# Attention features of batches 1 to 3: nine row blocks in three groups of three, each with its own bias

## The chip, the cores and the metric

The kernel runs on one core of a Trainium2 chip. The metric is the device time of one execution in microseconds (us); lower is better. The value for a kernel is the median of its runs.

## What is computed

Three stages follow each other. Random-feature attention on q, k, v of shape (4 batches, 8 heads, 576 rows, 64 columns) with 128 features, then two feed-forward stages on the 2304 rows of 512 columns that the attention gives.

```python
def phi(x):
    proj = np.einsum('bhsd,md->bhsm', x, omega)
    sq = np.sum(x * x, axis=-1, keepdims=True) / 2.0
    h = proj - sq
    h = h - np.max(h, axis=-1, keepdims=True)
    return np.exp(h) / np.sqrt(m)
q_p, k_p = (phi(q_s), phi(k_s))
kv = np.einsum('bhsm,bhsd->bhmd', k_p, v)
z = np.sum(k_p, axis=2)
num = np.einsum('bhsm,bhmd->bhsd', q_p, kv)
...
h = x @ w_in                                   # (2304, 512) @ (512, 2048)
g = h * (1.0 / (1.0 + np.exp(-1.702 * h)))
x = g @ w_out
...
out = ((x @ w_a) * (x @ w_b)) @ w_out2         # inner width 1536
```

The change touches how `phi` is cut into pieces; the numbers computed are the same.

## The kernel before

The attention works in phases. A phase is one pair of heads of one batch, for k (`kphase32`) or for q (`qphase`): 2 x 576 rows, cut into nine blocks of 128 rows. A batch has four k phases and four q phases. Batch 0 is done first and alone. The attention of batch b (1 to 3) is then run beside the first feed-forward stage of batch b-1 (`ffn1`), whose matmuls keep TensorE busy: the program is written as generators, and each unit of `ffn1` (twelve matmuls of 512 columns) is followed by one step of every attention phase that is live (`run`, `side_step`). A phase begins two steps after the one before it, so several phases are live together. Batch 1 keeps its features in float32 (`e32`), batches 2 and 3 split them into two float16 parts (`e16`). After the attention comes the second feed-forward stage (`ffn2`), which the change does not touch.

`features` (L374 on) is where `phi` is computed. For a group of blocks it takes one bank of PSUM from the pool `ps_att`, whose tag `att` has two banks for all live phases together; the products of the phase's end (`pk` in the k phase, `pn` twice in the q phase) and the transposes of batch 1 take banks of the same two. Into the bank go the projections (TensorE, L415 and L416, two matmuls of 128 columns for a block). VectorE takes the maximum of each row of each block (L481, one instruction for the group), and two small instructions (L487) turn it into the bias: `mh`, then `nb`, one column for a block. ScalarE then does one exponential for a block, straight from the bank (L447). When the last of them is done the bank is free. For batches 2 and 3, `parts` (L453) makes the two float16 parts of a group: one conversion on ScalarE (L457), one subtraction on VectorE (L458).

Before the change the nine blocks make groups of four, four and one. `PAIRS` says over which groups a bias is shared: group 0 has its own, groups 1 and 2 have one in common, which is made only when the maxima of both are there.

```python
GROUPS = [[0, 1, 2, 3], [4, 5, 6, 7], [8]]
PAIRS = [(0,), (1, 2), (1, 2)]
...
if gi - 1 == pair[-1]:
    for o, i0, scale in ((mh, mx, PROJ), (nb, mh, -1.0)):
        own["nb"] = nc.vector.scalar_tensor_tensor(...)
    for gj in pair:
        exps(gj, nb, a)
```

The steps are, before: (1) project group 0; (2) maximum, bias and exponentials of group 0, project group 1; (3) parts of group 0, maximum of group 1, project group 2; (4) maximum of group 2, shared bias, exponentials of groups 1 and 2; (5) parts of groups 1 and 2.

The order on each engine is not the order of the text. The framework's planner lays the instructions of each engine in a fixed order when the kernel is built: the text's order gives the priority, and the planner's own estimate of durations says when an operand or a buffer is there. At run time every engine follows that order and waits where something is late.

Other work on the same engines: VectorE converts weights from the raw form (`w_ops`, L215 to L263), does two instructions for each unit of `ffn1` (L667, L677) and the end of the q phases (L594 to L630). ScalarE does `th` and `gh` of `ffn1` (L664, L672, L676).

Of the kernel before, what the change touches and what calls it, by code (L numbers as in the profile page):

```python
# [9 lines left out]
F32 = mybir.dt.float32  # L10
F16 = mybir.dt.float16
I32 = mybir.dt.int32
AF = mybir.ActivationFunctionType
ALU = mybir.AluOpType
# [8 lines left out]
S_E = 2.0**13  # L23
# [11 lines left out]
def fused_kernel(  # L35
# [13 lines left out]
    nc = tc.nc  # L49
    B, H, S, D = q.shape  # L50
    M = omega.shape[0]
    DM, F1 = w_in_d.shape
    F2 = w_a_d.shape[1]
    P = 128
    NT = 4
# [6 lines left out]
    T = 2 * NT + 1  # L62
# [267 lines left out]


    raws = {}
    GROUPS = [[0, 1, 2, 3], [4, 5, 6, 7], [8]]
    PAIRS = [(0,), (1, 2), (1, 2)]
    GROUPS_F = [[0, 2, 4, 6], [1, 3, 5, 7], [8]]
    PAIRS_F = [(0, 1, 2)] * 3

# [29 lines left out]
    def places(g, shift):  # L367

        if not shift:
            return slice(g[0], g[-1] + 1)  # L370
        return slice(0, 1) if g[0] == 2 * NT else slice(g[0] + 1, g[-1] + 2)

    def features(pool, nm, x, e16, e32, psp, extra, shift=0):

        if nm[1] == "0":
# [3 lines left out]
            pt, pm = psp(), psp()  # L379
# [21 lines left out]
        else:  # L401
# [3 lines left out]
                out=x16[:, :, 1, :], in0=x, scalar=S_QK, in1=x16[:, :, 0, :],  # L405
                op0=ALU.mult, op1=ALU.subtract,
# [3 lines left out]
                out=xt, in_=x16.rearrange("p t j d -> p (t j d)")  # L410
# [28 lines left out]
        def exps(gi, nb, a):  # L439
            g, pv = groups[gi], pvs[gi]  # L440
            gs = slice(g[0], g[-1] + 1, 2 if len(g) > 1 and g[1] - g[0] == 2 else 1)
            if e32 is None:
                e = pool.tile([P, 4, M], F32, tag="e", name=f"e_{nm}_{gi}", bufs=2)
            else:
                e = e32[:, gs, :]
            for u, i in enumerate(g):
                nc.scalar.activation(  # L447
                    out=e[:, u, :], in_=pv[:, u, :], func=AF.Exp,
                    bias=nb[:, i - a : i - a + 1], scale=PROJ,
                )  # L450
            es[gi] = e

        def parts(gi):  # L453
            g, e = GROUPS[gi], es[gi]
            gs = places(g, shift)
            n = len(g)
            nc.scalar.activation(out=e16[:, 0, gs, :], in_=e[:, :n, :], func=AF.Copy, scale=S_E)  # L457
            nc.vector.scalar_tensor_tensor(  # L458
                out=e16[:, 1, gs, :], in0=e[:, :n, :], scalar=S_E, in1=e16[:, 0, gs, :],
                op0=ALU.mult, op1=ALU.subtract,  # L460
            )

        yield
        pvs, es, mxs, done = {}, {}, {}, []
        for gi in range(len(GROUPS) + 2):
            if e32 is None:
                for gj in [x for x in es if x not in done]:
                    parts(gj)
                    done.append(gj)
            if 1 <= gi <= len(GROUPS):  # L470
                g, pv = groups[gi - 1], pvs[gi - 1]
                pair = pairs[gi - 1]
                a, z = groups[pair[0]][0], groups[pair[-1]][-1] + 1
                ms = slice(g[0] - a, g[-1] + 1 - a, 2 if len(g) > 1 and g[1] - g[0] == 2 else 1)
                if pair[0] not in mxs:
                    mxs[pair[0]] = [
                        pool.tile([P, T], F32, tag=t, name=f"{t}_{nm}_{gi}", bufs=2)
                        for t in ("mx", "mh", "nb")
                    ]
                mx, mh, nb = mxs[pair[0]]  # L480
                nc.vector.tensor_reduce(  # L481
                    out=mx[:, ms], in_=pv[:, : len(g), :], axis=AX.X, op=ALU.max
                )
                if gi - 1 == pair[-1]:

                    for o, i0, scale in ((mh, mx, PROJ), (nb, mh, -1.0)):
                        own["nb"] = nc.vector.scalar_tensor_tensor(  # L487
                            out=o[:, : z - a], in0=i0[:, : z - a], scalar=scale, in1=sq[:, a:z],
                            op0=ALU.mult, op1=ALU.subtract,
                        ).ins  # L490
                    for gj in pair:
                        exps(gj, nb, a)
            if nm[1] == "0":
                if gi == 0:
                    for gj in range(len(GROUPS)):
                        pvs[gj] = psp().rearrange("p (t m) -> p t m", m=M)
                    project()
            elif gi < len(GROUPS):
                pvs[gi] = pv = psp().rearrange("p (t m) -> p t m", m=M)
                project(pv, GROUPS[gi])  # L500
            yield
# [46 lines left out]
    def qphase(pool, b, hp, xT, psp, nxt, f32=False):  # L548
        nm = f"q{b}_{hp}"
        bp, br = b % 2, b // 2  # L550
# [3 lines left out]
        if f32:  # L554
            e32 = pool.tile([P, T, M], F32, tag="e16", name=f"e32_{nm}")
            yield from features(pool, nm, raw, None, e32, psp, nxt)
            eq = pool.tile([P, T * P], F32, tag="eqT", name=f"eT32_{nm}")
            eT = eq.rearrange("p (t m) -> p t m", m=P)
            for gi, g in enumerate(GROUPS):
                pt = psp().rearrange("p (t m) -> p t m", m=M)  # L560
                for u, i in enumerate(g):
                    nc.tensor.transpose(pt[:, u, :], e32[:, i, :], own["ident"])
                cp = nc.vector.tensor_copy if gi in EVD else nc.scalar.copy
                cp(eT[:, places(g, 1 - bp), :], pt[:, : len(g), :])
            yield
            scale = 1.0

            def products(o, hh, c):
                nc.tensor.matmul(o, eq[:, c : c + P], own["kv"][:, hp, hh, :], start=True, stop=True)  # L569
        else:  # L570
            e16 = pool.tile([P, 2, T, P], F16, tag="e16", name=f"e16_{nm}")
            yield from features(pool, nm, raw, e16, None, psp, nxt, 1 - bp)
            TP = T * P
            eq = pool.tile([P, 2 * TP], F16, tag="eqT", name=f"eqT_{nm}")
            nc.sync.dma_start_transpose(
                out=eq.rearrange("p (l t m) -> p (l t) m", l=2, m=P),
                in_=e16.rearrange("p l t m -> p (l t m)"),
            )
            yield
            yield  # L580
            scale = S_E * S_KV

            def products(o, hh, c):
                lh, ll = eq[:, c : c + P], eq[:, TP + c : TP + c + P]
                nc.tensor.matmul(o, lh, kvh[:, hp, hh, :], start=True, stop=False)
                nc.tensor.matmul(o, lh, kvl[:, hp, hh, :], start=False, stop=False)
                nc.tensor.matmul(o, ll, kvh[:, hp, hh, :], start=False, stop=True)
# [31 lines left out]
        if b == 0:  # L619
            pt = psp()  # L620
# [4 lines left out]
        else:  # L625
# [5 lines left out]
            out=x16r[rows, br, 1, hp, :], in0=xr, in1=x16r[rows, br, 0, hp, :], op=ALU.subtract  # L631
        )
        yield
        if b:
            nc.sync.dma_start_transpose(
                out=xT[:, hp].rearrange("p l (t c) -> p (l t) c", t=NT),
                in_=x16.rearrange("p l t c -> p (l t c)"),
# [630 lines left out]
```

## Time and profile before

| | |
|---|---|
| median of 3 runs | 897.92 us (897.53 to 898.5) |
| span of the profiled execution (first to last instruction), which is its own time within 0.1 us of the lowest run | 897.5 us |
| TensorE (PE) busy | 874.1 us, 97% |
| VectorE (DVE) busy | 674.2 us, 75% |
| ScalarE (ACT) busy | 457.6 us, 51% |
| mean granted TensorE clock | 0.995 |

How to read it: the profile gives for each engine the time in which it executes something. Matmuls overlap in their pipe, so a matmul of 512 columns has a record of about 0.38 us while the next one starts 0.215 us after it; a busy TensorE can therefore hide short waits. A wait is idle time of an engine before an instruction, put down to whatever ended it. The stretches used below are: up to 79 us mostly batch 0, 79 to 184 us batch 1 beside `ffn1` of batch 0, 184 to 290 us batch 2 beside `ffn1` of batch 1, 290 to 388 us batch 3 beside `ffn1` of batch 2, then the rest of `ffn1`, and `ffn2` from about 485 us.

### The profile page before, as it was taken

What the parts mean: (1) busy time and instruction counts of PE and PEld (TensorE: products, weight loads), DVE (VectorE), ACT (ScalarE), POOL (GpSimd) and SP (SyncE); (2) the same over time, 40 slices, a digit from 0 to 9 for tenths busy, and PEclk for the clock granted to TensorE, in tenths of its full rate; (3) what the DMA queues carried; (4) which work ended last, traced back from release to release, by engine and by line L of the source; (5) the groups of instructions that cost most, each with busy time, mean ns of one, the idle gap of its engine ahead of it and who ended that gap; (6) DMA issues with size and microseconds to landing.
All of it is one profiled execution on the core that took longest, in us unless ns stands there. A gap on an engine that the chain in (4) does not pass through costs nothing.

```text
span 897.5 us, 17366 instructions
## 1 busy us (share of the span) xinstructions
PE 874.1 (97%) x7094; PEld 628.0 (70%) x7094; DVE 674.2 (75%) x1212; ACT 457.6 (51%) x1088; POOL 1.4 (0%) x10
## 2 busy tenths in 40 slices
PE   8999999999999999999999999999999999999997
PEld 6874655645554455444448888888888889888886
DVE  4889999787797787999611179987999557566766
ACT  6777875677656775564323354544443122233221
POOL 0000000000000000000000000000000000000000
PEclk8999999999999999999999999999999999999999
DMA  6945886344674314785401045232332022223312
GB/s 174 251 143 163 223 209 218 95 124 92 129 172 118 74 28 80 136 269 223 141 1 48 16 138 175 108 89 83 130 130 81 3 42 85 83 95 129 77 49 71
DMA packets 129343, 105.35 MB, mean 117 GB/s; under 512 B 97776, under 2 KB 111088, under 8 KB 127216
## 3 DMA queue, kind: packets, MB, share of 16 engines
q1 hardware_dynamic: 128558, 103.66, 41.0%
q8 instruction: 55, 0.90, 0.4%
q10 hardware_dynamic: 706, 0.59, 0.2%
q14 instruction: 24, 0.20, 0.1%
HBM read 71.07 MB, written 17.69 MB: 99 GB/s over the span
## 4 chain that ended last, share of the span: by engine, by line
PE 66%; DVE 17%; ACT 7%; DMA 4%; issue 2%; ACTq 0%; SPq 0%
PE y L690 4%; PE ph L655 4%; PE ph L656 4%; PE y L691 4%; PE ph L657 4%; PE y L692 4%; DMA xt_k<-x_k 3%; PE oA L912 2%; PE oA L910 2%; PE pbA L816 2%; PE pbA L814 2%; PE pbA L815 2%; PE oA L911 2%; PE pa L569 2%; PE paA L814 2%; PE paA L816 2%
## 5 line engine op out<-in xcount | busy, mean ns | idle before, releaser
L691 PE MATMUL y<-gl,w_out 128*128 128x512 f16 (+1 forms) x320 | 114.4, 358 | 0.6 <-DVE gl L677 0.4
L692 PE MATMUL y<-gh,w_out 128*128 128x512 f16 (+1 forms) x320 | 114.3, 358 | 0.0
L690 PE MATMUL y<-gh,w_out 128*128 128x512 f16 (+1 forms) x320 | 112.3, 358 | 0.7 <-ACT gh L676 0.7
L677 DVE SCALAR_TENSOR_TENSOR gl<-th,gh 128x512 f16<-128x512 f32 (+1 forms) x80 | 50.7, 635 | 66.6 <-ACT gh L676 66.3
L655 PE MATMUL ph<-xT,w_in 128*128 128x512 f16 x256 | 97.0, 379 | 1.5 <-DMA xT<-x_q_3x 0.7
L656 PE MATMUL ph<-xT,w_in 128*128 128x512 f16 x256 | 97.0, 379 | 0.3 <-DVE xT L624 0.3
L657 PE MATMUL ph<-xT,w_in 128*128 128x512 f16 x256 | 97.0, 379 | 0.0
L814 PE MATMUL paA<-forms,w_a 128*128 128x256 f16 (+1 forms) x240 | 61.0, 262 | 1.6 <-DVE ca L835 1.3
L814 PE MATMUL pbA<-forms,w_b 128*128 128x256 f16 (+1 forms) x240 | 61.0, 262 | 0.7 <-DVE cb L835 0.7
L816 PE MATMUL pbA<-forms,w_b 128*128 128x256 f16 (+1 forms) x240 | 61.0, 262 | 0.0
L815 PE MATMUL pbA<-forms,w_b 128*128 128x256 f16 (+1 forms) x240 | 61.0, 262 | 0.0
L816 PE MATMUL paA<-forms,w_a 128*128 128x256 f16 (+1 forms) x240 | 61.0, 262 | 0.0
L815 PE MATMUL paA<-forms,w_a 128*128 128x256 f16 (+1 forms) x240 | 61.0, 262 | 0.0
L912 PE MATMUL oA<-w_o,ab 128*128 128x256 f16 x216 | 58.9, 273 | 0.6 <-DVE ab L868 0.5
L910 PE MATMUL oA<-w_o,ab 128*128 128x256 f16 x216 | 58.9, 273 | 0.1
L911 PE MATMUL oA<-w_o,ab 128*128 128x256 f16 x216 | 58.9, 273 | 0.0
L676 ACT ACTIVATE gh<-th 128x512 f16<-128x512 f32 (+1 forms) x80 | 47.1, 589 | 23.0 <-DVE th L667 22.0
L824 ACT COPY ka<-paA 128x512 f32<-128x512 f32 (+1 forms) x30 | 16.3, 544 | 82.1 <-PE paA L816 82.1
L918 DVE SCALAR_TENSOR_TENSOR o<-oA,o 128x512 f32<-128x512 f32 (+1 forms) x45 | 28.4, 633 | 33.6 <-PE oA L912 33.6
L692 PEld LDWEIGHTS <-w_out 128*128 128x128 f16 x320 | 31.4, 98 | 29.3 <-issue 1.9
L657 PEld LDWEIGHTS <-w_in 128*128 128x128 f16 x320 | 31.5, 98 | 28.7 <-DVE w_in L222 1.1
L690 PEld LDWEIGHTS <-w_out 128*128 128x128 f16 x320 | 31.5, 99 | 28.6 <-issue 1.2
(211 smaller groups left out, 2373.8 us busy)
## 6 DMA issues: line engine op xcount, KB each, us to landing
wraw<-in_moe_w_out_dram SPq DMA_DIRECT2D x14, 1024.0 KB
forms<-fd SPq DMA_DIRECT2D x8, 1792.0 KB
wraw<-in_moe_w_in_dram SPq DMA_DIRECT2D x8, 1024.0 KB
fd<-forms SPq DMA_DIRECT2D x4, 1792.0 KB
wraw<-in_moe_w_a_dram SPq DMA_DIRECT2D x6, 1024.0 KB
wraw<-in_moe_w_b_dram SPq DMA_DIRECT2D x6, 1024.0 KB
vt<-in_v_dram SPq DMA_DIRECT2D x16, 256.0 KB
rawq<-in_q_dram SPq DMA_DIRECT2D x16, 256.0 KB
```

The costliest lines, as they stand in the source:

```text
L655: nc.tensor.matmul(ph[:, :n], w[:, 0, c, fs], xh(c), start=(c == 0), stop=False)
L656: nc.tensor.matmul(ph[:, :n], w[:, 0, c, fs], xl(c), start=False, stop=False)
L657: nc.tensor.matmul(ph[:, :n], w[:, 1, c, fs], xh(c), start=False, stop=(c == KC - 1))
L690: nc.tensor.matmul(o, w[:, 0, f % 4, cs], gh[f][:, :n], start=(f == 0), stop=False)
L691: nc.tensor.matmul(o, w[:, 0, f % 4, cs], gl[f][:, :n], start=False, stop=False)
L692: nc.tensor.matmul(o, w[:, 1, f % 4, cs], gh[f][:, :n], start=False, stop=(f == FC1 - 1))
L814: nc.tensor.matmul(o[:, i], wh, xh, start=first, stop=False, skip_group_check=True)
L815: nc.tensor.matmul(o[:, i], wh, xl, start=False, stop=False, skip_group_check=True)
L816: own["pe"] = nc.tensor.matmul(o[:, i], wl, xh, start=False, stop=final, skip_group_check=True).ins
L910: nc.tensor.matmul(bank[:, t], lh, wh, start=first, stop=False, skip_group_check=True)
L911: nc.tensor.matmul(bank[:, t], lh, wl, start=False, stop=False, skip_group_check=True)
L912: nc.tensor.matmul(bank[:, t], ll, wh, start=False, stop=final, skip_group_check=True)
```

## The change

Batches 1 to 3 use three groups of three blocks, each with a bias of its own. The tile `e` shrinks from four blocks to three, the small tiles `mx`, `mh` and `nb` get three buffers in place of two. The transposes of batch 1's q features keep the groups of four, four and one (`GROUPS_T`). Where a q phase puts block 8 in front of the others (the shift, batch 2), the last group is converted in two pieces, blocks 6 and 7 and block 8.

```diff
--- before.py
+++ after.py
@@ -330,8 +330,9 @@
 
 
     raws = {}
-    GROUPS = [[0, 1, 2, 3], [4, 5, 6, 7], [8]]
-    PAIRS = [(0,), (1, 2), (1, 2)]
+    GROUPS_T = [[0, 1, 2, 3], [4, 5, 6, 7], [8]]
+    GROUPS = [[0, 1, 2], [3, 4, 5], [6, 7, 8]]
+    PAIRS = [(0,), (1,), (2,)]
     GROUPS_F = [[0, 2, 4, 6], [1, 3, 5, 7], [8]]
     PAIRS_F = [(0, 1, 2)] * 3
 
@@ -367,8 +368,12 @@
     def places(g, shift):
 
         if not shift:
-            return slice(g[0], g[-1] + 1)
-        return slice(0, 1) if g[0] == 2 * NT else slice(g[0] + 1, g[-1] + 2)
+            return [(slice(0, len(g)), slice(g[0], g[-1] + 1))]
+        n = sum(i < 2 * NT for i in g)
+        runs = [(slice(0, n), slice(g[0] + 1, g[0] + 1 + n))] if n else []
+        if n < len(g):
+            runs.append((slice(n, n + 1), slice(0, 1)))
+        return runs
 
     def features(pool, nm, x, e16, e32, psp, extra, shift=0):
 
@@ -440,7 +445,7 @@
             g, pv = groups[gi], pvs[gi]
             gs = slice(g[0], g[-1] + 1, 2 if len(g) > 1 and g[1] - g[0] == 2 else 1)
             if e32 is None:
-                e = pool.tile([P, 4, M], F32, tag="e", name=f"e_{nm}_{gi}", bufs=2)
+                e = pool.tile([P, 3, M], F32, tag="e", name=f"e_{nm}_{gi}", bufs=2)
             else:
                 e = e32[:, gs, :]
             for u, i in enumerate(g):
@@ -452,13 +457,12 @@
 
         def parts(gi):
             g, e = GROUPS[gi], es[gi]
-            gs = places(g, shift)
-            n = len(g)
-            nc.scalar.activation(out=e16[:, 0, gs, :], in_=e[:, :n, :], func=AF.Copy, scale=S_E)
-            nc.vector.scalar_tensor_tensor(
-                out=e16[:, 1, gs, :], in0=e[:, :n, :], scalar=S_E, in1=e16[:, 0, gs, :],
-                op0=ALU.mult, op1=ALU.subtract,
-            )
+            for us, gs in places(g, shift):
+                nc.scalar.activation(out=e16[:, 0, gs, :], in_=e[:, us, :], func=AF.Copy, scale=S_E)
+                nc.vector.scalar_tensor_tensor(
+                    out=e16[:, 1, gs, :], in0=e[:, us, :], scalar=S_E, in1=e16[:, 0, gs, :],
+                    op0=ALU.mult, op1=ALU.subtract,
+                )
 
         yield
         pvs, es, mxs, done = {}, {}, {}, []
@@ -474,7 +478,7 @@
                 ms = slice(g[0] - a, g[-1] + 1 - a, 2 if len(g) > 1 and g[1] - g[0] == 2 else 1)
                 if pair[0] not in mxs:
                     mxs[pair[0]] = [
-                        pool.tile([P, T], F32, tag=t, name=f"{t}_{nm}_{gi}", bufs=2)
+                        pool.tile([P, T], F32, tag=t, name=f"{t}_{nm}_{gi}", bufs=3)
                         for t in ("mx", "mh", "nb")
                     ]
                 mx, mh, nb = mxs[pair[0]]
@@ -556,12 +560,13 @@
             yield from features(pool, nm, raw, None, e32, psp, nxt)
             eq = pool.tile([P, T * P], F32, tag="eqT", name=f"eT32_{nm}")
             eT = eq.rearrange("p (t m) -> p t m", m=P)
-            for gi, g in enumerate(GROUPS):
+            for gi, g in enumerate(GROUPS_T):
                 pt = psp().rearrange("p (t m) -> p t m", m=M)
                 for u, i in enumerate(g):
                     nc.tensor.transpose(pt[:, u, :], e32[:, i, :], own["ident"])
                 cp = nc.vector.tensor_copy if gi in EVD else nc.scalar.copy
-                cp(eT[:, places(g, 1 - bp), :], pt[:, : len(g), :])
+                ((_, gs),) = places(g, 1 - bp)
+                cp(eT[:, gs, :], pt[:, : len(g), :])
             yield
             scale = 1.0
 
```

## Rows read from the trace of the kernel before

**Rows 1.** The page's part 1: busy us, share of the span, instructions.

```profile
PE 874.1 (97%) x7094; PEld 628.0 (70%) x7094; DVE 674.2 (75%) x1212; ACT 457.6 (51%) x1088; POOL 1.4 (0%) x10
```

**Rows 2.** Windows: stretch, its length, busy of PE, PEld, DVE, ACT; clock, DMA share.

```profile
79.00:184.00 105.00, 102.45 (x644) 59.47 (x644) 92.37 (x164) 73.23 (x253) 0.00 (x0) 1.00 0.69 189
184.00:290.00 106.00, 102.47 (x761) 52.55 (x760) 85.77 (x197) 74.91 (x182) 0.00 (x0) 1.00 0.56 122
290.00:388.00 98.00, 93.80 (x721) 48.53 (x719) 81.17 (x187) 61.07 (x155) 0.00 (x0) 1.00 0.44 89
```

**Rows 3.** Waits of PE from 79 to 400 us: us in total, times, longest.

```profile
PE pa L415 <- ACT e_k L447: 1.8, 1, 1.8
PE pa L415 <- DVE sx L249: 1.3, 1, 1.3
PE pa L529 <- DVE sx L249: 1.0, 1, 1.0
...
PE ph L655 <- DMA xT<-x_q_3x: 0.7, 1, 0.7
PE pa L529 <- ACT e_q L447: 0.6, 3, 0.2
PE pa L415 <- ACT e_q L447: 0.6, 2, 0.4
PE pa L529 <- ACT e_k L447: 0.4, 1, 0.4
PE y L691 <- DVE gl L677: 0.4, 1, 0.4
PE pa L415 <- DVE kvl L505: 0.3, 2, 0.2
...
PE pa L585 <- ACT e_q L447: 0.2, 1, 0.2
```

**Rows 4.** Timeline, one q phase of batch 2: start us, us, instruction, idle before.

```profile
242.42 0.22 PE L415 MATMUL pa<-om_h,xt_q 128*128 128x128 f16 x1
...
243.34 0.69 DVE L481 TENSOR_REDUCE mx_q<-pa 128x4 f32<-128x512 f32 x1
...
244.21 0.69 DVE L481 TENSOR_REDUCE mx_q<-pa 128x4 f32<-128x512 f32 x1
...
245.09 1.14 ACT L447 ACTIVATE e_q<-pa,nb_q 128x128 f32<-128x128 f32 x4 [2.19 <-DVE nb_q L487]
...
245.67 0.38 PE L690 MATMUL y<-gh,w_out 128*128 128x512 f16 x1
...
246.28 0.22 PE L415 MATMUL pa<-om_h,xt_q 128*128 128x128 f16 x1 [0.23 <-ACT e_q L447]
...
248.98 1.40 ACT L447 ACTIVATE e_q<-pa,nb_q 128x128 f32<-128x128 f32 x5 [0.84 <-DVE nb_q L487]
...
250.17 0.22 PE L415 MATMUL pa<-om_h,xt_q 128*128 128x128 f16 x1
```

**Rows 5.** VectorE's groups by shape: xcount, busy us, mean ns of one.

```profile
L481 DVE TENSOR_REDUCE mx_q<-pa 128x4 f32<-128x512 f32 x32 | 21.8, 687 | 5.1 <-PE pa L416 4.7
...
L481 DVE TENSOR_REDUCE mx_q<-pa 128x1 f32<-128x128 f32 x16 | 4.6, 287 | 3.2 <-PE pa L416 3.1
...
L487 DVE SCALAR_TENSOR_TENSOR nb_q<-mh_q,sq_q 128x4 f32<-128x4 f32 x12 | 1.9, 156 | 0.0
```

**Rows 6.** ScalarE's groups by shape: conversions of the features (L457).

```profile
L457 ACT ACTIVATE e_q<-e_q 128x512 f16<-128x512 f32 x16 | 10.2, 640 | 0.8 <-PE pa L531 0.6
...
L457 ACT ACTIVATE e_q<-e_q 128x128 f16<-128x128 f32 x8 | 2.6, 330 | 0.0
```

**Rows 7.** Windows around the end of batch 3, columns as in rows 2.

```profile
375.00:425.00 50.00, 48.76 (x243) 22.02 (x240) 49.06 (x84) 28.43 (x47) 0.00 (x0) 1.00 0.71 230
425.00:450.00 25.00, 25.00 (x118) 11.36 (x116) 16.44 (x23) 8.02 (x13) 0.00 (x0) 1.00 0.37 127
450.00:500.00 50.00, 50.00 (x359) 34.86 (x357) 7.43 (x15) 15.97 (x34) 0.00 (x0) 1.00 0.06 22
```

## The prediction

> **What bounds the kernel.** The engine totals come first: TensorE is busy 874.1 of 897.5 us, VectorE 75%, ScalarE 51% [rows 1]. So the end is set by TensorE's queue, and a change that leaves the matmuls alone can only move what TensorE waits. The projections are 9 blocks x 2 matmuls in a phase before and after; nothing is taken from or added to its work. The windows by stage then say how much waiting there is where the change acts: TensorE idles 105.00 - 102.45 = 2.6 us beside batch 1, 106.00 - 102.47 = 3.5 us beside batch 2 and 98.00 - 93.80 = 4.2 us beside batch 3, 10.3 us in all [rows 2]. No gain from this change can be much larger than that.
>
> The list of TensorE's waits says who ends them [rows 3]. A projection (L415), the k product (L529) or the q product (L585) that waits for the exponentials L447 is waiting for a bank of PSUM: its operands are long there, and the exponentials are the last readers of a bank. These rows give 1.8 + 0.6 + 0.6 + 0.4 + 0.2 = 3.6 us in 8 waits. Two more waits of the same two lines end with a VectorE instruction that has nothing to do with them (sx, 1.3 + 1.0 us), two with kvl (0.3 us); I count these four as bank waits as well, since the maximum and the bias stand in the same VectorE queue as those instructions. That makes 6.2 us in 12 waits. A wait is listed shorter than it is: in the one at 246.28 the last matmul started at 245.67, the next could have started 0.215 us later, so TensorE stood 0.39 us where 0.23 is listed [rows 4]. With 0.16 us for each of 12, the bank waits are about 8.1 us.
>
> The timeline of one q phase shows why the banks are late [rows 4]. Groups 0 and 1 are projected together by 242.8. Group 0's exponentials end at 245.09 + 1.14 = 246.23, and its bank is taken at once, at 246.28, for block 8. Group 1's maximum is done at 244.90, but its bias is shared with block 8, which must wait for that bank; so the five exponentials of both come at 248.98 to 250.38. The fourth ends some 0.25 us before the fifth, at about 250.13, and the next phase's projection takes the bank at 250.17. Group 1 held its bank for 7.7 us, about four of them only for the shared bias. It is also to be seen that the planner puts the projection right at the release, in the middle of a unit of the feed-forward stage (between L690 and the L691 that belongs to it): TensorE waits because the real release comes later than the planned one.
>
> **The change, part by part.**
>
> Maxima: 2 x 687 + 287 = 1661 ns for a phase before [rows 5]. No row has 384 columns; on the line through the two shapes it is 287 + 256 x (400 / 384) = 554 ns, three times 1662 ns. Bounds are 287 and 687 for one; the line is taken because both ends lie on the same instruction. Cost zero.
>
> Bias: two instructions more for each of 24 phases, 48 x 156 ns = 7.5 us of VectorE [rows 5]. VectorE has 12.6, 20.2 and 16.8 us idle in the three stretches [rows 2], so this is taken as hidden there; its price without that cover is the third rival. On the path of a group it costs nothing new: each group had to have a bias, now it has one of its own.
>
> Exponentials: nine for a phase as before, in runs of three. A run of four takes 1.14 us, of five 1.40 us [rows 4], so one of three about 0.88 us.
>
> Parts (batches 2 and 3): 2 x 640 + 330 = 1610 ns on ScalarE before [rows 6]; three of 384 columns on the line, 3 x (330 + 256 x 310 / 384) = 1610 ns. Equal, and likewise on VectorE. Only the four q phases of batch 2 pay more: the last group goes in two pieces, one more instruction on each engine. By the step that such an instruction costs beyond its columns (330 - 128 x 0.81 = 226 ns) that is 0.9 us of ScalarE, and at most 4 x 287 = 1.1 us of VectorE. Both have idle time beside it [rows 2]; zero on the path, at most 2.0 us if none of it is covered.
>
> Buffers: the tile e is smaller, the bias tiles have three buffers for three groups as they had two for two. No DMA is added or moved, and no queue gets a new wait. The transposes of batch 1 stay in fours; they come when all exponentials of their phase are done, so the new grouping does not hold them up.
>
> Banks: this is where the gain is. Counted from 242.4 for the first two, the three groups hold a bank before to 246.2, to 250.1 and from 246.3 to 250.4, about 3.8 + 7.7 + 4.1 = 15.6 us [rows 4]. After, group 0 saves 0.13 us of maximum and 0.26 us of exponentials: 3.4 us. Group 1 no longer waits for block 8: its maximum and bias follow group 0's, its three exponentials follow group 0's three, so I put it at 4.7 us. The last group is three blocks: its maximum is 0.27 us longer and its run of exponentials 0.52 us shorter than five, about 3.9 us. Sum 12.0 us, 23% less. The rest of the cycle (products, parts) is not shortened. What this does to the waits no row shows. At the one end all of the 8.1 us go, at the other nothing goes, because the planner simply places the projections at the new, earlier release. I take a share like that of the bank time, about 30% with the waits that disappear because a bank is already free when TensorE comes to it: 8.1 x 0.3 = 2.4 us. The wait at the end of batch 3, for the last transposed x (0.7 listed, 0.86 real) [rows 3], gets smaller when that batch's attention is through earlier; half of it, 0.4 us.
>
> Sum: -2.4 - 0.4 = -2.8 us. The profiled execution spans 897.5 us, 0.4 below the median of 897.92; the difference is applied to the median: **895.1 us**. About 0.2% (1.8 us) is what a measurement of this kernel tells from no change, so the forecast is only just outside it. Its own range is 0.9 us (a tenth of the waits gone) to 6 us (two thirds gone) of gain: 892 to 897.
>
> **The rivals.**
>
> The waits stay (25%). The planner's order is just in time before and just in time after; the lateness of the real chain against the planned one is what TensorE waits, and a group still has one maximum, two bias instructions and a run of exponentials. There are also more places: pairs of projections that now go back to back after a common release get a release each. Then the time is 897.9, within 1 us or so. For it speaks that most waits are 0.1 to 0.4 us [rows 3], against it that group 1's bank clearly waits on the shared bias [rows 4].
>
> VectorE becomes the late one (20%). The place is the end of batch 3 and the start of `ffn1` of that batch: from 375 to 425 us VectorE is busy 49.06 of 50 us [rows 7]. TensorE already waits there for gl [rows 3]. Batch 3's eight phases bring 16 x 0.156 = 2.5 us more of bias work; if VectorE is the bound from there on, these go into TensorE's waits for gl one for one, and the gain at the banks is lost behind the same queue: 897.9 + 2.5 = 900.4 us. If all 48 had to be paid it would be 905.4. It decides when VectorE has no idle time left before TensorE's next unit needs it. Against it: weight conversions can slip, since VectorE has 8.6 of 25 and then 42.6 of 50 us free from 425 to 500 us [rows 7]. The Trainium skill (Perfetto Trace Analysis, Optimizing Scalar/DVE Operations) says that grouping into larger operations improves throughput where the engine is saturated, with about 60 ns of fixed cost for a VectorE operation on SBUF. By that figure the 48 added operations would be an estimated 2.9 us in all and not 7.5; in this stretch the trace has the engine at 98%, so by that rule this rival's sign holds, its size would be smaller.
>
> The banks stop being the limit (9%). With 23% less bank time for a phase the two banks may nearly always be free when TensorE arrives. Then all of the 8.1 us and the 0.86 us at the end of batch 3 go: 888.9 us. Against it: the phases are run closer together as soon as banks allow, and the wait for them comes back.
>
> **How the numbers follow.** Forecast 46%, waits stay 25%, VectorE late 20%, banks free 9%. Faster by over 0.2% is the forecast and the last: 0.55. Within 0.2%: 0.25. Slower: 0.20. The range must reach from the better part of the last case to the third's price: 890.5 to 900.4 us; outside lie about half of the 9% and the part of the third case that pays for more than batch 3, together some 15%.
>
> **What would show it.** Right: in the timeline of a q phase of batch 2 group 1's exponentials follow group 0's within about 2 us, the bank waits in the list of 79 to 400 us fall from 6.2 us to about 4, the idle time of TensorE in the three stretches sums to about 8 us, `ffn2` is as before. The number of L487 instructions is larger by 48. Wrong: the same sum of idle time (waits stay); waits of the feed-forward lines L655 to L692 for gl, gh and th growing by over 2 us (VectorE late); or waits that arise after 400 us, since the planner may lay out the later work in another order too.

## The result and the profile after

The changed kernel takes 906.81 us (median of four runs, 904.09 to 908.72) where the kernel before takes 898.11 (897.53 to 898.50): a ratio of 1.0094, 95% interval 1.0069 to 1.0119. It is slower by 8.7 us. The forecast was 895.1 us, the range 890.5 to 900.4.

The profiled execution of after took 908.72 us with a span of 906.9, that of before a span of 897.5; the two traces differ by 9.4 us. In the runs on record that have both, the time is 1.8 us above the span, so the trace of before, by an estimate from these, is of an execution of about 899.3 us and not of the lowest run. Page, part 1, of after, beside [rows 1]:

```profile
PE 876.9 (97%) x7094; PEld 628.4 (69%) x7094; DVE 676.4 (75%) x1264; ACT 458.7 (51%) x1092; POOL 1.4 (0%) x10
```

The matmuls are as many as before, VectorE has the 48 bias instructions and the four split parts more (1264 - 1212 = 52), 2.2 us of busy time in all. Work did not make the kernel longer; waiting and the clock did.

**Where it is lost.** The output copies `ye` (L704 before, L709 after) of each feed-forward tile are marks that both timelines have. ScalarE's timelines, first `ye` of the four tiles, before:

```profile
176.00 2.13 ACT L704 ACTIVATE ye<-y 128x512 f32<-128x512 f32 x4
...
284.98 1.07 ACT L704 ACTIVATE ye<-y 128x512 f32<-128x512 f32 x2
...
391.77 0.59 ACT L704 ACTIVATE ye<-y 128x512 f32<-128x512 f32 x1
...
472.00 2.45 ACT L704 ACTIVATE ye<-y 128x512 f32<-128x512 f32 x4
```

and after:

```profile
177.23 2.04 ACT L709 ACTIVATE ye<-y 128x512 f32<-128x512 f32 x4
...
288.77 0.60 ACT L709 ACTIVATE ye<-y 128x512 f32<-128x512 f32 x1
...
396.53 0.59 ACT L709 ACTIVATE ye<-y 128x512 f32<-128x512 f32 x1
...
481.52 2.45 ACT L709 ACTIVATE ye<-y 128x512 f32<-128x512 f32 x4
```

After is late by 1.2, 3.8, 4.8 and 9.5 us. But the two traces are not level where the changed phases begin. The first matmul of `ffn1` starts, before and then after, at

```profile
57.14 0.38 PE L655 MATMUL ph<-xT,w_in 128*128 128x512 f16 x1
```

```profile
55.27 0.38 PE L660 MATMUL ph<-xT,w_in 128*128 128x512 f16 x1
```

so after is 1.9 us ahead there. Up to that point nearly all work is that of batch 0, which the change leaves alone. The trace of before ran at the lower clock in its first part (window, columns as in rows 2):

```profile
8.00:15.00 7.00, 6.72 (x43) 5.72 (x44) 4.38 (x9) 4.16 (x12) 0.00 (x0) 0.51 0.86 180
```

In after the granted clock is 1.00 there. This belongs to the execution and not to the kernel: the experiments e2, e8, e9 and e11 below, whose batches 0 and 1 are as in before, start `ffn1` at 54.74, 54.76, 56.31 and 56.35 us, with none, none, 3.4 and 3.4 us at the lower clock ahead of it. Counted from the start of `ffn1`, after loses 3.1 us with batch 1, 2.6 with batch 2, 1.0 with batch 3, and 4.7 between 392 and 472 us of before, where the attention is over: 11.4 us. Behind that nothing more is lost.

Windows of after: the three stretches of [rows 2], the one behind them, and three short ones (columns as in rows 2):

```profile
79.00:184.00 105.00, 102.42 (x634) 59.48 (x634) 91.39 (x177) 73.83 (x242) 0.00 (x0) 0.98 0.73 186
184.00:290.00 106.00, 99.34 (x737) 51.07 (x736) 84.60 (x213) 70.52 (x177) 0.00 (x0) 0.98 0.54 109
290.00:388.00 98.00, 94.06 (x723) 48.98 (x721) 82.65 (x204) 64.42 (x161) 0.00 (x0) 1.00 0.48 104
388.00:485.00 97.00, 93.82 (x440) 43.20 (x438) 57.08 (x87) 39.71 (x66) 0.00 (x0) 0.98 0.40 134
81.00:84.50 3.50, 3.50 (x14) 1.58 (x14) 2.82 (x7) 1.95 (x5) 0.00 (x0) 0.52 0.44 84
262.00:265.50 3.50, 3.38 (x22) 1.73 (x23) 0.76 (x2) 0.00 (x0) 0.00 (x0) 0.51 0.57 112
408.50:412.50 4.00, 4.00 (x12) 1.47 (x11) 4.00 (x6) 1.69 (x3) 0.00 (x0) 0.57 0.12 48
```

TensorE's idle time beside batches 1 to 3 is 2.6 + 6.7 + 3.9 = 13.2 us, where it was 10.3. But there is a second loss that idle time does not show: in three of the stretches the granted clock, 1.00 before, is 0.98, and all of it lies in the three short windows, where TensorE runs at the lower of its two levels, 1.2 GHz. Each costs about 1.7 us of work that is done at half speed: 3.5 x 0.48, 3.5 x 0.49, 4.0 x 0.43. The Trainium skill (TensorE: Matmul & The Clock Gate, Part 1) reckons the price of the lower clock in the same way, as the time spent there times one half. The trace agrees in so far as matmuls of 512 columns start 0.41 us apart there (shown below) and 0.215 us elsewhere.

The list of TensorE's waits, after, 79 to 400 us, beside [rows 3], then 400 to 420 us, where before has none:

```profile
PE pa L590 <- DMA eqT_q<-e_q: 3.3, 2, 2.6
PE pa L420 <- ACT e_k L452: 3.1, 5, 1.5
PE pa L533 <- ACT e_k L452: 1.7, 2, 1.2
PE pa L533 <- DVE x_q L409: 1.2, 1, 1.2
PE pa L420 <- ACT e_q L452: 1.1, 4, 0.4
...
PE pa L420 <- DVE sx L249: 0.2, 1, 0.2
...
PE y L695 <- ACT gh L681: 2.4, 1, 2.4
PE y L696 <- DVE gl L682: 0.3, 1, 0.3
```

Before has one line for `eqT` in its list from 79 to 400 us as well, which [rows 3] leave out:

```profile
PE pa L585 <- DMA eqT_q<-e_q: 0.7, 1, 0.7
```

It stands at 370.86 us, in batch 3, and is the other one (0.7 us) of the two in the first line of after. Two long waits are new. One, 2.6 us, is the q product L590 waiting for the transposed features `eqT`; the other, 2.4 us, is L695 waiting for `gh` behind the end of the attention. Behind each stands one of the half-clock stretches. The bank waits, counted as in the prediction, are 3.1 + 1.7 + 1.2 + 1.1 + 0.2 = 7.3 us in 13, where they were 6.2 in 12.

**The first new wait: the load in front of the transpose.** SP's queue, after, where the last `eqT` of batch 2 is issued:

```profile
252.81 0.39 SPq L201 DMA_DIRECT2D wraw<-in_moe_w_b_dram  x1
254.46 5.20 SPq L580 DMA_TRANSPOSE eqT_q<-e_q  x1
```

and before:

```profile
261.35 0.38 SPq L201 DMA_DIRECT2D wraw<-in_moe_w_b_dram  x1
263.94 3.27 SPq L575 DMA_TRANSPOSE eqT_q<-e_q  x1
```

The same weight load of 1 MB stands in front of the transpose in both, 2.59 us ahead before and 1.65 us ahead after. With less distance the transpose sits on the queue for 5.20 us in place of 3.27. TensorE's timeline, after, shows what came of it:

```profile
262.12 0.23 PE L590 MATMUL pa<-kvh,eqT_q 128*128 128x65 f16 x1 [2.60 <-DMA eqT_q<-e_q]
...
262.94 0.62 PE L662 MATMUL ph<-xT,w_in 128*128 128x512 f16 x1
263.35 0.63 PE L660 MATMUL ph<-xT,w_in 128*128 128x512 f16 x1
```

The product starts 262.12 - 254.46 = 7.7 us behind the issue, and the matmuls of 512 columns behind it start 0.41 us apart, not 0.215: the lower clock. In the kernel before the product came 4.7 us behind the issue (268.59 - 263.94), with no wait listed for this `eqT`. In after the DMA moves 381, 373 and 256 GB/s from 255 to 258 us, behind the issue of the transpose; that these bytes are the load's is read from their place, the view does not name them.

**The second: the load in front of the stores.** At the end of tile 2 the four `ye` are stored through SP. Before:

```profile
392.39 3.22 SPq L705 DMA_DIRECT2D yd<-ye  x4
397.01 0.38 SPq L201 DMA_DIRECT2D wraw<-in_moe_w_b_dram  x1
```

After:

```profile
397.65 0.37 SPq L201 DMA_DIRECT2D wraw<-in_moe_w_b_dram  x1
398.07 2.65 SPq L710 DMA_DIRECT2D yd<-ye  x4
```

The load now stands ahead of all four stores. ScalarE, after:

```profile
405.46 0.60 ACT L677 ACTIVATE th<-ph 128x512 f32<-128x512 f32 x1 [3.07 <-DMA yd<-ye]
```

`th` and `ye` share four buffers (tag f32). With the stores late, `th` has none for 3.07 us, `gh` follows it, and TensorE, which takes `gh`, stands.

The account of the traced execution, the slowest of the four: 2.6 for `eqT`, 2.4 + 0.3 for `gh` and `gl`, 3 x 1.7 for the clock make 10.4 of the 11.4 us lost from the start of `ffn1` on. About 1 us is left for all else, and the slow start of the trace of before takes 1.9 off the difference of the spans. The parts do not meet stage by stage: beside batch 2 the wait and the clock make 4.3 us where 2.6 are lost, beside batch 3 1.0 us is lost with neither.

### The profile page after: what moved, and what is told of

It is laid out like the page before. It is cut to its first block, busy times and chain, and to the rows that moved or that the text cites. A ratio compares the mean times of both kernels' runs of the same rounds, so it can differ in the third digit from the quotient of the medians.

```text
span 906.9 us, 17446 instructions
## 1 busy us (share of the span) xinstructions
PE 876.9 (97%) x7094; PEld 628.4 (69%) x7094; DVE 676.4 (75%) x1264; ACT 458.7 (51%) x1092; POOL 1.4 (0%) x10
## 4 chain that ended last, share of the span: by engine, by line
PE 64%; DVE 16%; ACT 8%; DMA 7%; issue 2%; ACTq 0%; SPq 0%
PE ph L662 4%; PE ph L660 4%; PE ph L661 4%; PE y L695 4%; PE y L696 4%; PE y L697 4%; PE oA L917 2%; PE oA L915 2%; PE pbA L821 2%; PE pbA L819 2%; PE pbA L820 2%; PE oA L916 2%; PE pa L574 2%; PE paA L819 2%; PE paA L821 2%
## 5 line engine op out<-in xcount | busy, mean ns | idle before, releaser
L695 PE MATMUL y<-gh,w_out 128*128 128x512 f16 (+1 forms) x320 | 112.5, 360 | 2.8 <-ACT gh L681 2.6
L660 PE MATMUL ph<-xT,w_in 128*128 128x512 f16 x256 | 98.3, 384 | 0.7 <-DVE th L672 0.7
L661 PE MATMUL ph<-xT,w_in 128*128 128x512 f16 x256 | 98.1, 383 | 0.3 <-DVE xT L629 0.3
L662 PE MATMUL ph<-xT,w_in 128*128 128x512 f16 x256 | 98.1, 383 | 0.0
L697 PEld LDWEIGHTS <-w_out 128*128 128x128 f16 x320 | 31.4, 98 | 29.9 <-issue 3.0
```

Source lines behind the costliest of these rows:

```text
L660: nc.tensor.matmul(ph[:, :n], w[:, 0, c, fs], xh(c), start=(c == 0), stop=False)
L661: nc.tensor.matmul(ph[:, :n], w[:, 0, c, fs], xl(c), start=False, stop=False)
L662: nc.tensor.matmul(ph[:, :n], w[:, 1, c, fs], xh(c), start=False, stop=(c == KC - 1))
L695: nc.tensor.matmul(o, w[:, 0, f % 4, cs], gh[f][:, :n], start=(f == 0), stop=False)
L697: nc.tensor.matmul(o, w[:, 1, f % 4, cs], gh[f][:, :n], start=False, stop=(f == FC1 - 1))
```

## The experiments

Twelve kernels, each beside runs of the kernel before on the same chip. Each has one trace, of one execution. The changed kernel itself was not run again beside them, so it is compared by its ratio to before. The first four split the change.

**Groups of three in one part of the batches only.**

```diff
-        groups, pairs = (GROUPS_F, PAIRS_F) if nm[1] == "0" else (GROUPS, PAIRS)
+        groups, pairs = (GROUPS, PAIRS) if nm[1] in "1" else (GROUPS_O, PAIRS_O)   # "1": e1; "23": e2
+        if nm[1] == "0":
+            groups, pairs = GROUPS_F, PAIRS_F
...
```

> Only batch 1 has the groups of three, batches 2 and 3 keep four, four and one. Theory A (the loss comes from three single long waits that the new order of the program makes, each followed by 3.4 us at half clock, and has no price that belongs to a group of three): what batch 1 does alone is the wait near 81 us with its clock fall, about 1.6 + 1.7 us, and whatever new order the later work gets: anywhere from 897 to 905 us. Theory B (a group of three with its own bias costs a fixed sum for each phase, 8.7 us over 24 phases): 8 phases of 24 are changed, 898.1 + 2.9 = 901.0 us.

Measured: 900.46 against 898.30 us, 1.0019 (1.0002 to 1.0036).

> Only batches 2 and 3 have the groups of three. Theory A: the wait near 81 us is that of the kernel before, no clock fall there; the waits near 262 us (last q product on its transpose) and 407 us (y on gh) come again only if the planner lays the same order; 897 to 906 us, and the time above 898 us is found in at most three waits of over 1 us and in clock falls. Theory B: 16 phases of 24, 898.1 + 5.8 = 903.9 us, spread evenly over the phases.

Measured: 902.68 against 898.30 us, 1.0062 (1.0043 to 1.0080). Both parts lose. The times alone do not tell a price for each phase (901.0 and 903.9 us were expected by it) from single waits; that rests on the traces. e1 has the wait for `eqT` (2.7 us, in batch 2, where its grouping is as before) and the lower clock there and at 83 us. In e2 the first `ye` of tile 2 comes about 1 us earlier than in before (390.82 against 391.77); but its `ffn1` began 2.4 us earlier (54.74 against 57.14), so 1.4 us are lost up to there. Then it loses over 4 us at one place. TensorE's waits of e2, 400 to 420 us:

```profile
PE y L698 <- ACT gh L684: 2.2, 1, 2.2
PE y L699 <- DVE gl L685: 0.4, 1, 0.4
```

with a granted clock of 0.58 from 401 to 405 us behind them. ScalarE waits 3.07 us for `yd<-ye` there, as in after; SP has the load at 391.76 and the four stores from 392.18. So groups of three in batches 2 and 3 alone were no gain up to 391 us either, and most of the loss is the second new wait. The lower clock is not the whole of it: three of the seven runs of e2 have a mean granted clock of 1.000 and took 901.82, 902.21 and 903.15 us.

**Own biases with the old groups, and groups of three with shared biases.**

```diff
-    GROUPS = [[0, 1, 2], [3, 4, 5], [6, 7, 8]]      # e3: groups 4, 4, 1, each with its own bias
+    GROUPS = GROUPS_T
...
-    PAIRS = [(0,), (1,), (2,)]                      # e4: groups of three, the last two share a bias
+    PAIRS = [(0,), (1, 2), (1, 2)]
```

> Groups of four, four and one as before, but each with a bias of its own: 48 more bias instructions on VectorE, and a bank of the second group is free earlier. If the 48 bias instructions are what costs, as the rival with VectorE late has it: 903 to 907 us, as with the change. If the size of the groups is what costs: 898 us within 1 us. Theory A: neither; the time follows from where single long waits fall, 896 to 905 us.

Measured: 901.33 against 898.30 us, 1.0051 (1.0031 to 1.0070).

> Groups of three with one bias shared by the last two: no more bias instructions than before. If the 48 bias instructions cost: back to 898 to 899 us. If the groups of three cost: 905 to 908 us, or more, since two full banks are now held for the common bias. Theory A: 897 to 908 us, set by single long waits of over 1 us and the clock falls behind them.

Measured: 905.38 against 898.30 us, 1.0079 (1.0054 to 1.0105). The kernel without the 48 added bias instructions (e4) is slower than the one that has them (e3), so their number is not the cost. That e4 lands at 905 to 908 us is also what was expected if the groups of three cost in themselves, and its trace does not put the loss at the two loads: `eqT` is waited for 1.72 us with no lower clock behind it, `th` waits 0.91 us for the stores, and 4.2 of its 7.3 us counted from the start of `ffn1` are lost up to the first `ye` of tile 0, beside batch 1. What costs in e4 was not followed up. e3 has the wait for `eqT` too. Its TensorE timeline:

```profile
261.58 0.20 PE L590 MATMUL pa<-kvh,eqT_q 128*128 128x65 f16 x1 [3.17 <-DMA eqT_q<-e_q]
...
262.05 0.38 PE L660 MATMUL ph<-xT,w_in 128*128 128x512 f16 x1
262.26 0.38 PE L661 MATMUL ph<-xT,w_in 128*128 128x512 f16 x1
```

The wait for `eqT` does not come from the size of the groups. And here it is longer than in after, 3.17 us, yet the matmuls behind it start 0.21 us apart: no lower clock.

**The weight load put behind what it delayed.** In the loader of the weights, applied to the changed kernel:

```diff
+            hold = own.get("yd2" if i >= NWE + 4 else "eqT")
+            with tc.issue_after(hold) if hold else ExitStack():
                 nc.sync.dma_start(out=t, in_=src)
...
+            if b == 2 and hp == NHP - 1:          # e5, e7, e8
+                own["eqT"] = dma.ins              # the last eqT of batch 2
...
+                        if j == 2:                # e6, e7, e8
+                            own["yd2"] = dma.ins  # the fourth store of tile 2
```

> The changed kernel with one 1 MB weight load issued behind the last eqT transpose of batch 2 in place of in front of it; nothing else is asked for. Theory A (a load planned in front of a transfer that an engine needs soon makes that transfer late, and the long wait is followed by half clock): TensorE's wait of 2.6 us near 262 us and the clock fall behind it go, about 4.3 us: 902.5 us, range 901 to 904. Theory C (the transpose is late for another reason, say because the attention now ends earlier and the planner's order is too tight): the wait stays within 0.5 us of 2.6, 906 to 908 us.

Measured: 903.38 against 897.55 us, 1.0063 (1.0039 to 1.0088).

> The changed kernel with one 1 MB weight load issued behind the four stores of y of the third ffn1 tile in place of in front of them. Theory A: ScalarE's wait of 3.1 us for the stores (th needs a buffer that ye holds) goes, with it TensorE's 2.4 + 0.35 us for gh and gl near 407 us and the clock fall of 1.7 us: 906.8 - 4.5 = 902.3 us, range 901 to 904. Theory C: the stores land as late as before, 906 to 908 us.

Measured: 902.43 against 897.55 us, 1.0044 (1.0021 to 1.0068).

> Both orders of the two runs before. Theory A: both gains, 906.8 - 8.8 = 898.0 us, range 896.5 to 900, with one clock fall left, near 81 us. Theory B (the groups of three cost in themselves): at least 903 us, since only two places are mended.

Measured: 900.84 against 897.55 us, 1.0033 (1.0010 to 1.0055). SP's queue in e5:

```profile
251.72 3.31 SPq L580 DMA_TRANSPOSE eqT_q<-e_q  x1
255.07 0.59 SPq L203 DMA_DIRECT2D wraw<-in_moe_w_b_dram  x1
```

The transpose is back at 3.31 us, the wait for it at 1.16 (it was 2.60; TensorE now comes to the product 4.2 us behind the issue and starts it at 5.35, where before it started at 4.65 without a wait), and no half clock follows in the traced execution, the fastest of the twelve. In e6 the four stores are issued from 395.77 us and the loads from 399.08, and its list of TensorE's waits from 400 to 420 us is empty. Both orders together leave 0.33% of the 0.94%: about 3 us of 8.4 (ratios times 898). The other 5 to 6 us are these two places, with the lower clock where it follows. The interval of both orders (up to 1.0055) lies clear of that of the change (from 1.0069). That of the stores alone ends just below it (1.0068), that of the transpose alone overlaps it (1.0088), so the time does not show the transpose's share by itself. e5 and e6 came out as expected; e7 is 0.8 us above its range of 896.5 to 900, which means that something is left beside the two places.

> The kernel before with the same two orders: its load stands in front of the transpose too (2.6 us ahead, with a wait of 0.2 us), and behind the stores already. Theory A: 897.5 to 898.5 us, the same within 0.2%. If the two orders are a gain of their own, whatever the groups: clearly under 896 us, and then what the run with both shows is not the mending of the change's loss.

Measured: 898.00 against 897.55 us, 1.0000 (0.9978 to 1.0023). The kernel before gains nothing from the same two orders; they mend what the change brought.

**A load put in front of the stores in the kernel before.** A copy of 1 MB from DRAM to DRAM is added between the first and the second store of tile 2; nothing uses its result.

```diff
+                        if j == 2 and c == 0:
+                            front = ydram.tile([P, 2048], I32, tag="front", name="front")
+                            with tc.issue_after(dma.ins):
+                                own["front"] = nc.sync.dma_start(
+                                    out=front, in_=w_in_d.bitcast(I32)[0:128, 0:2048]
+                                ).ins
...
```

> The kernel before, with one added transfer of 1 MB from memory to memory between the first and the second of the four stores of y of the third ffn1 tile; its result is used by nobody. Theory A (a large load in front of these stores keeps ye's buffers, ScalarE waits for them with th, TensorE with y): a wait of ScalarE for the stores of 2 to 4 us and of TensorE for gh of 1.5 to 3 us near 400 us, in some runs a clock fall: 897.5 + 2 to 5 = 899.5 to 902.5 us. Theory C (the loss near 407 us belongs to the new groups, not to the load): 897.5 us within 1 us, as the copy is off every engine's path.

Measured: 898.91 against 897.89 us, 1.0010 (0.9999 to 1.0020): a miss. ScalarE in e9:

```profile
398.06 0.60 ACT L672 ACTIVATE th<-ph 128x512 f32<-128x512 f32 x1 [0.23 <-DMA yd<-ye]
```

It waits 0.23 us, not 3. The first store was issued ahead of the copy; that it freed the buffer is likely but not shown. A large load among the stores is not enough to make the wait. The traces order it by the place of the load: ahead of all four stores by 0.42 us, `th` waits 3.07 us in after and e2 and 2.57 in e5; ahead of all four by 1.40 us, 1.01 (e3); behind the first store, 0.91 (e4) and 0.23 (e9); behind all four, no wait.

**The two orders with one part of the change** (the edits of e1 and e5, and of e2 and e7, together):

> Groups of three in batch 1 alone, and the weight load behind the last eqT transpose of batch 2. Theory A: the wait of 2.7 us near 268 us goes, and the clock fall where there is one: 900.5 - 3 = 897.5 us, range 896 to 899, the same as the kernel before. Theory B (a price for each phase with groups of three): 900 us or more.

Measured: 899.98 against 897.89 us, 1.0011 (0.9993 to 1.0030). More than was expected: the long wait for `eqT` is gone (0.2 us listed), but a wait of 1.1 us for `e_q` came instead, and the clock is 0.51 from 83.5 to 87 us. The time lies at the mark of the price for each phase (900 us or more). Against e1 (1.0019), with overlapping intervals, the order bought nothing that can be told.

> Groups of three in batches 2 and 3, both loads behind their transfers. Theory A: without the wait near 401 us (2.4 + 0.5 us and a clock fall of 1.7) 902.7 - 4.5 = 898.2 us, range 897 to 900; the bank waits between 184 and 400 us stay at 13 us, as in the run without the two orders. If the shorter holds of the banks do pay once the late transfers are out of the way: 896 us or less.

Measured: 899.72 against 897.89 us, 1.0022 (1.0012 to 1.0032), within what was expected. The wait at 401 us is gone with its half clock (granted 1.00 from 401 to 405 us); some 2 us remain, and the granted clock of its trace is 1.00 from 12 to 898 us.

**A third buffer for the halves of x**, on top of e7, to see whether the remaining bank waits come from ScalarE's conversions L408, which stand in its queue in front of the exponentials and wait for a transpose to free their buffer. Room for it was made by one raw q buffer less.

```diff
-    RAW = {"k": 3, "q": 4}
+    RAW = {"k": 3, "q": 3}
...
-            x16 = pool.tile([P, T, 2, D], F16, tag="A", name=f"x16_{nm}")
+            x16 = pool.tile([P, T, 2, D], F16, tag="A", name=f"x16_{nm}", bufs=3)
...
```

> The changed kernel with both loads behind their transfers, and a third buffer for x16 (paid for by one buffer less for the raw q tiles, whose loads come later for it). Theory D (what is left of the loss, 3 us, are bank waits that grew because runs of three exponentials stand on ScalarE behind conversions of x that wait for a transpose to release their buffer): ScalarE's waits of L408 for DMA fall from 7 us to under 4, TensorE's bank waits from 19 to 16 us, and the time to 898.5 us, range 897 to 900. Theory W (the waits are the planner's lateness at each take-over of a bank, of which there are some more): ScalarE's waits for DMA fall, the bank waits stay at 18 to 19 us, 900 to 901.5 us.

Measured: 899.93 against 897.62 us, 1.0025 (1.0013 to 1.0037). ScalarE's waits in e7 and then in e12:

```profile
ACT x_k L408 <- DMA xt_k<-x_k: 2.6, 3, 1.2
```

```profile
ACT x_k L408 <- DMA rawk<-in_k_dram: 3.1, 2, 2.1
```

The waits for the transposes get shorter (2.6 and 2.2 us in e7 for x of k and q, 0.6 in all in e12), but others took their place: now the conversions wait for the raw loads. The ratio against e7 cannot be told from none (1.0025 and 1.0033, with intervals that overlap nearly whole). TensorE's bank waits, counted as above, are 7.2 us in e7's trace and 5.7 in e12's; the 16 to 19 us of the expectation are counted otherwise. 899.93 us lies at the upper end of the one range and just below the other. What the last 2 to 3 us are is not settled by it.

## Why the prediction was wrong

**The step that failed: "No DMA is added or moved, and no queue gets a new wait."** The diff moves none, but the order of SP's queue is the planner's, and the transposes and stores came to stand elsewhere against the weight loads: one load nearer in front of a transpose, one ahead of four stores that it had followed. What needed the transpose and the buffers of the stores was then some 3 us late. That the q phases of batch 2 follow each other faster (their four transposes are spread over 25.5 us in after, 229.0 to 254.5, and over 29.9 in before) may be part of why; it is not shown, and e1, whose batch 2 has the old groups, has the same wait. The prediction itself had "the planner may lay out the later work in another order too" among what would make it wrong, but gave it neither a price nor a chance.

The traces order the first of the two by the time that the load is ahead of the transpose on SP:

| kernel | load ahead, us | transpose on SP, us | wait of TensorE, us |
|---|---|---|---|
| after | 1.65 | 5.20 | 2.60 |
| e6 | 1.65 | 5.38 | 2.78 |
| e1 | 1.75 | 5.19 | 2.66 |
| e3 | 1.95 | 4.66 | 3.17 |
| e2 | 2.25 | 4.04 | 0.71 |
| before | 2.59 | 3.27 | none |
| e9 | 2.59 | 4.07 | 0.95 |
| e4 | 2.86 | 3.52 | 1.72 |
| e5 | behind | 3.31 | 1.16 |
| e8 | behind | 2.69 | none |

The Trainium skill (DMA: Bandwidth & Descriptors, Queues, rings and completion order) says that the transfers issued by one engine share a ring on each DMA engine, which takes its descriptors in order. The table fits that: behind a load 1.65 to 2.25 us ahead the transpose takes 4.0 to 5.4 us, behind one 2.6 to 2.9 us ahead 3.3 to 4.1, and with no load in front 2.7 to 3.6 (e5, e7, e8, e10 to e12). The load is not all that lengthens one: in after another transpose of batch 2, 42 us behind the last load, takes 4.48 us. And TensorE's wait does not follow the table: it hangs as well on when TensorE comes to the product, and differs from one execution to the next (before and e9 have the same order there).

**A price that no term had: the clock.** The sum took a wait for what it lasts. In the traced execution of after each of three places of waiting is followed by 3.5 us at 1.2 GHz, another 1.7 us each and 5.1 in all. Not every execution pays that: the four runs differ by 4.6 us, and the fastest, at a mean granted clock of 0.998, is still 6.0 us slower than before. So the clock makes the loss larger and uneven, and it is not the greater part of it in every run. At the third place the only new thing listed is the form of the wait: one of 1.76 us at 81.35 before [rows 3] became two, 0.79 and 1.46 us, at 79.04 and 80.99. Of the seven traces with this pair (after, e1, e5, e6, e7, e10, e12) five have the lower clock behind it, all but e5 and e12; of the five with the single wait (before, e2, e8, e9, e11) none has.

**"a share like that of the bank time, about 30%": wrong, the rival that the waits stay was right here.** The term of -2.4 us had the holds nearly right and the waits wrong. ScalarE's timeline of a q phase of batch 2, after, beside [rows 4]:

```profile
234.28 1.66 ACT L452 ACTIVATE e_q<-pa,nb_q 128x128 f32<-128x128 f32 x6 [2.00 <-DVE nb_q L491]
```

The exponentials of two groups come in one run of six, to 235.94. Their projections were at 231.34 and 232.64, so they hold a bank for about 3.8 and 3.3 us; the group projected ahead of them, at 227.12, has its exponentials done at 231.29, 4.2 us. These are three groups in sequence and not one phase. Over the eleven groups projected from 220 to 249 us a bank is held 4.3 us on average, 12.8 for three, where the forecast was 12.0 and the phase that the prediction read had 15.6. The sign in the exponentials (group 1's within 2 us behind group 0's) holds in one of three q phases: 0.7, 3.5 and 3.8 us. But the waits did not fall with the holds (7.3 us in 13, from 6.2 in 12), and TensorE's idle time in the three stretches rose to 13.2 us where about 8 were forecast. That the planner uses the earlier release to place the next phase earlier, so that TensorE still waits for the lateness of the real chain against the planned one, fits this and is not shown. Some of the waiting lies in work queued ahead of the exponentials. All engines, after, at 323 us:

```profile
322.75 0.68 ACT L408 ACTIVATE x_q<-rawq 128x576 f16<-128x576 f32 x1 [1.14 <-DMA xt_q<-x_q]
...
323.85 0.86 ACT L452 ACTIVATE e_k<-pa,nb_k 128x128 f32<-128x128 f32 x3
...
324.77 0.22 PE L533 MATMUL pa<-v_k,e_k 128*128 128x130 f16 x1 [1.24 <-ACT e_k L452]
```

The conversion of the next x waits 1.14 us for a transpose, and the exponentials stand behind it. The Trainium skill (Perfetto Trace Analysis, Optimizing Scalar/DVE Operations) says that breaking up instructions may let work be completed sooner when the engine is not saturated but causes bubbles elsewhere. The first half is what the trace shows, in the shorter holds; TensorE's waits stayed.

**The rival of a late VectorE: wrong in its cause, right in its sign.** The wait at 407 us is in the place that it named, and its sign (waits for `gl`, `gh` and `th` up by over 2 us) came true, but the wait comes from the stores; of its 2.7 us only 0.3 end with VectorE, and e4, which has no added bias, loses most among the first four.

**Right:** the maximum of 384 columns (554 ns estimated, 551 measured), the bias at its size (154 ns) and hidden, the wait for the last transposed x of batch 3 (0.7 us listed before) gone, `ffn2` unchanged. VectorE's group of the new shape, after (columns as in rows 5):

```profile
L485 DVE TENSOR_REDUCE mx_q<-pa 128x3 f32<-128x384 f32 x36 | 19.6, 551 | 4.5 <-PE pa L421 4.5
```

**What stays open.** With both orders mended some 2 to 3 us remain (e7, e11, e12). Part of it stands beside batch 1: counted from the start of `ffn1` to the first `ye` of tile 0, the seven traces with the pair of waits near 80 us lose 1.1 to 5.1 us against before, the four others whose batch 1 is as before 0.1 to 1.2. The lower clock there is in some executions and not in others, and bank waits are longer; neither was changed alone. e11, with the old batch 1, still loses 2 us, with no lower clock behind a wait in its trace. No version that ran was faster than the kernel before. Why the two loads come to stand where they do in the planner's reckoning was not followed up.

## What to carry to other kernels

Where a planner lays out the queues, a change of one piece's length re-lays the order everywhere behind it: compare the DMA queues of the two kernels for large loads that came in front of a transpose, or of stores whose buffers are wanted soon. Price a new TensorE wait of a few microseconds at what it lasts and, as the worse case, at half of the stretch at the lower clock that may follow (here 1.7 us). A resource that is released earlier shortens the kernel only where the wait for it gets shorter too; here it did not. Before two traces are subtracted, compare them where the change has not yet acted: here one was 1.9 us ahead.

## What was not expected of the hardware

The same wait does and does not cost the clock. A wait of 2.60 us (after) was followed by 3.5 us at a granted clock of 0.51, one of 3.17 us (e3) by none. The two waits near 80 us stand in e5 as in after; TensorE, e5:

```profile
78.54 0.22 PE L420 MATMUL pa<-om_h,xt_k 128*128 128x128 f16 x1 [0.81 <-ACT e_k L452]
...
80.49 0.22 PE L420 MATMUL pa<-om_h,xt_k 128*128 128x128 f16 x1 [1.46 <-ACT e_k L452]
...
81.22 0.38 PE L664 MATMUL ph<-xT,w_in 128*128 128x512 f16 x1
81.44 0.38 PE L662 MATMUL ph<-xT,w_in 128*128 128x512 f16 x1
```

and the matmuls behind them start 0.22 us apart, where after has 0.43. At the stores the waits of 2.4 + 0.35 us (after) and 2.2 + 0.35 (e2) were followed by the lower clock, those of 1.87 + 0.35 in e5 were not. So the length of a wait alone does not tell it. The four runs of the changed kernel lie 4.6 us apart, and their mean granted clock goes with the time: 904.09 us at 0.998, 905.38 at 0.996, 908.24 and 908.72 at 0.994.
